# Loading v of batches 0 and 1 in place, w_out by row pairs, and a new set of priorities in a fused attention and feed-forward kernel

## The chip, the cores and the metric

The kernel runs on one core of a Trainium2 chip. It is timed in device microseconds (us) for one execution, inputs and outputs in the chip's memory. A second number is the span of a profiled execution, from the program's first instruction to its last. The engines are named PE (TensorE matmuls), PEld (its weight loads), DVE (VectorE), ACT (ScalarE), POOL (GpSimd) and SP (SyncE). POOL and SP here mostly issue DMAs: POOL the loads that convert float32 to bfloat16, SP the stores, the DMA transposes and two plain loads.

## The reference

There are 8 batches of 8 heads, 576 positions and 64 features. Heads 0 to 3 attend to the last 32 positions; heads 4 to 7 attend to every fourth position of the last 128. The result, as 4608 rows of 512, goes through a feed-forward block.

```python
scores = scale * np.matmul(q, k.transpose(0, 1, 3, 2))
mask_plain = (rel >= 0) & (rel < window)                                    # window 32
mask_dil = (rel >= 0) & (rel < window * dilation) & (rel % dilation == 0)   # dilation 4
attn = softmax(np.where(mask, scores, -1e9))
x = np.matmul(attn, v).transpose(0, 2, 1, 3).reshape(B * S, H * D)
a = x @ w1            # w1, w2: 512 x 1024
b = x @ w2
h = a * b @ w3        # w3: 1024 x 1024
out = h @ w_out       # w_out: 1024 x 512
```

## The kernel before

**Algebra.** The two last products are made one: `w3 @ w_out` is computed once on the chip into `wf_sb`, in eight parts. A part is a load of 128 rows of w3, eight PE transposes of it ("W3T", `w3_back`), an ACT copy to `w3T`, eight matmuls against `wo_sb` ("W3M", `w3_mul`) and a copy to `wf_sb` ("W3D").

**Attention.** A batch has two units u: the plain heads (u=0) and the dilated ones (u=1), and each has six blocks of 96 queries. q and k are loaded by rows (`load_rows`, a contiguous run for each partition) and turned on DVE in 32x32 blocks into `qt` and `kt` (`turn`, "Tqn", "Tkn"). For scores ("S"), 8 small matmuls per block go to PSUM. In batch 0 four groups of three blocks are formed, and the mask is added by four matmuls against `bias` ahead of each; from batch 1 on a group has five blocks and DVE multiplies by a mask ("M"). ACT takes the exponentials ("E"). A step is half a unit: 12 matmuls of `et` with v and a column of ones ("V"), a reciprocal ("R"), a normalization ("N"), and a way back to feature-major order in `XT`. For batches 0 and 1 that way is six PE transposes ("X", `back`) and a copy ("K", `keep`); later it is a DMA transpose on SP.

**v.** `vps` are two buffers of 128 partitions: partitions 32 to 127 hold a block's 96 positions, and partitions 0 to 31 hold the 32 before them (the halo). From batch 2 on (`DIRECT_V = 2`) one DMA for the plain heads and eight for the dilated ones load v straight into place, 256 bytes of float32 at a time (`load_v_plain`, `load_v_dil`), and one DVE copy fills the halo (`halo_v`). For batches 0 and 1 v comes by rows, is turned on DVE, transposed on PE in four parts of six transposes ("VT", `v_back`) and copied to `vps` ("VK", `v_keep`).

**Feed-forward.** A unit of 288 rows is half a batch. For each of eight 128-wide slices f of d_ff come four matmuls for a and four for b ("UP", line 563), an ACT copy of a and a DVE product into `gt` (line 578). For each 128 rows of output eight matmuls follow ("DOWN", line 589), a copy and a store. The first sixteen slices alternate: slices 0 to 3 of units 0 and 1, then slices 4 to 7 of both.

**Order.** Every piece of work is a task with an engine, an assumed duration, dependencies and a priority. `Plan.run` plays these through once as the program is built, and the resulting order is fixed for each engine. Durations and priorities therefore change nothing but the order. If PE would be idle in that play before its first UP, it gets filler matmuls ("fill", line 701). Loads go out on POOL in the order of `B0_LOADS`, then `FIRST_LOADS`, then by batch; POOL also builds the masks (`MASK_AT` sets their place among the loads). Completion semaphores of POOL's loads are used in turn, eight of them: a load is issued when the eighth one before it has landed. q and k of batch 0, u=0, are loaded by SP as float32 into `gt` and rounded by ACT (`round_rows`, "C").

Of the kernel before, what the change touches and what calls it, by code (L numbers as in the profile page):

```python
# [10 lines left out]
P = 128  # L11
# [19 lines left out]
LATE = False  # L31
TURNED = 2
DIRECT_V = 2
ORDER = (2, 3, 0, 1)
RES = (0, 2, 1, 3)
RANK = dict(E=0.5, VK=3, K=2, N=0.2, T=0.5, VT=0.05, S=0.1, V=0.05, X=0.1, W=0.5, C=5)
FIRST = {"E": 3, "VK": 1, "K": 0.2, "N": 2, "T": 0.2, "VT": 0.05, "S": 0.3, "V": 0.1, "X": 0.3}
WARM = 25
FILL = 110
FIRST_LOADS = ("30", "w0", "v10", "w1", "w2", "31", "k10", "q10", "o0", "o1", "32", "33", "34", "q11", "k11", "v11", "35", "36", "37")  # L40
SHIFT = {}
ON_DVE = ("K0.2", "VK0.1.1", "W3D1", "W3D4", "W3D5")
GRP = 5
WHOLE = ("qn", "kn")
B0_LOADS = ("v0", "q1", "k1", "v1")
HALVED = ("K0.0", "K0.1", "K0.3", "K1.1", "VK0.0.0", "VK0.1.0", "VK1.0.1", "VK1.1.0")
MASK_AT = 19.5
PARTED = 0
BUSY = 4500
LEAD = 1.1  # L50
# [13 lines left out]
class Plan:  # L64
# [15 lines left out]
    def run(self):  # L80
# [42 lines left out]
        while len(order) < n:  # L123
            progress = True
            while progress:
                progress = False
                for e in engines:
# [31 lines left out]
                    else:  # L159
                        t.end = free[e] = now + t.dur  # L160
# [26 lines left out]
def kernel(  # L187
# [75 lines left out]
    def round_rows(nm, u, half):  # L263
# [14 lines left out]
        nc.scalar.copy(out=o, in_=i)  # L278
# [26 lines left out]
    def halo_v(b):  # L305
        vp = vps[b % 2]
        nc.vector.tensor_copy(out=vp[0:32, :, 1:6, 0:D], in_=vp[96:128, :, 0:5, 0:D])
# [6 lines left out]
    def load_wo(c):  # L314
        g = slice(4 * c, 4 * c + 4)
        nc.gpsimd.dma_start(
            out=wo_sb[:, g, :],
            in_=moe_w_out[512 * c : 512 * (c + 1), :].rearrange("(a p) f -> p a f", p=P),
        )
# [155 lines left out]
    class Step:  # L475
# [51 lines left out]
        def back(self):  # L527
            self.x = bank(6 * QB, BF16)
            for i in range(6):
                nc.tensor.transpose(  # L530
                    out=self.x[:, i * QB : (i + 1) * QB],
                    in_=self.xo[0:QB, i * P : (i + 1) * P],
                    identity=ident[0:QB, 0:QB],
                )
# [109 lines left out]
    def w3_back(ft):  # L644
        x = bank(KFF * P, BF16).rearrange("p (g x) -> p g x", g=KFF)
        for g in range(KFF):
            nc.tensor.transpose(  # L647
                out=x[:, g, :], in_=w3n[ft][:, g * P : (g + 1) * P], identity=ident
            )
# [70 lines left out]
    def loads_rows(nm, b, us=None):  # L720
# [4 lines left out]
        t = load(f"L{nm}{b}", 700, 3100 if us is None else 1600, old,  # L725
# [4 lines left out]
    def loads_v(b):  # L730
        old = vdone.get(b - 2, [])
        LV[b] = [load(f"LP{b}", 1300, 4700, old, lambda: load_v_plain(b))]
        LV[b] += [
            load(f"LD{b}.{m}", 600 if m % 3 != 1 else 1200, 770, old, lambda m=m: load_v_dil(b, m))
            for m in range(6)
        ]

    WC = (slice(0, 256), slice(256, 512), slice(512, 1024))

    def loads_w12(c):  # L740
        return [
            load("LW", 800, (1700, 1700, 3300)[c], [], lambda d=d, s=s: load_w(d, s, WC[c]))
# [3 lines left out]
    for i, nm in enumerate(WHOLE):  # L746
        t = add(f"LF{nm}", "SP", 100, [], lambda nm=nm: load_whole(nm, rows_of[nm], 0), -9 + i,
                lat=4400 + 1350 * i)
        L[(nm, 0, 0)] = [
            add(f"C{nm}.{half}", "ACT", 650, [t], lambda nm=nm, h=half: round_rows(nm, 0, h),  # L750
                -9 + i + 0.1 * half, lat=100)
            for half in range(2)
        ]
    plan.dma = 1200 + 1350 * len(WHOLE)
    for x in B0_LOADS:
        loads_rows(x[0] + "n", 0, (int(x[1]),))
# [10 lines left out]
    for x in FIRST_LOADS:  # L767
# [3 lines left out]
        elif x[0] == "o":  # L771
            lwo[c] = load(f"LWO{c}", 600, 3300, [], lambda c=c: load_wo(c))
        elif x[0] == "3":
            lw3[c] = load(f"LW3.{c}", 550, 1400, [], lambda ft=c: load_w3(ft))
        elif x[0] == "v" and DIRECT_V <= c:
            loads_v(c)
# [21 lines left out]
    def turns(b, u, nm, pr):  # L798
# [4 lines left out]
        else:  # L803
            parts = (2, 3, 4, 5) if b == 0 else (0, 1)
# [16 lines left out]
    for b in range(B):  # L821
# [9 lines left out]
        for u in range(2):  # L831
# [3 lines left out]
            for half in range(2):  # L835
# [6 lines left out]
                eng, dur = ("DVE", 980) if name in ON_DVE else ("ACT", 880)  # L842
                ways = [(eng, dur, slice(0, 4))]
                if name in HALVED:
                    ways = [("ACT", 540, slice(0, 2)), ("DVE", 560, slice(2, 4))]
                vals[(b, u, half)] = [
                    add(name, e, dur, [x, c0],
                        lambda b=b, u=u, h=half, e=e, hs=hs: v_keep(b, u, h, e, hs),
                        10 * b + rank("VK", b), lat=100)
                    for e, dur, hs in ways  # L850
                ]
        if b >= DIRECT_V:
            hal = add(f"HALO{b}", "DVE", 820, LV[b] + [c0], lambda b=b: halo_v(b), 10 * b + 2,
                      lat=80)
            for u in range(2):
                for half in range(2):
                    vals[(b, u, half)] = [hal] + LV[b]


        def group(blocks, biased):  # L860
# [6 lines left out]
            if biased:  # L867
                s = add("S" + n, "PE", 980, need + [blk, idt], lambda: g.scores(True),
                        b - 99 + rank("S", b), slot=4)
                e = add("E" + n, "ACT", 1150, [s], g.exps, 10 * b + rank("E", b), lat=100, after=old)  # L870
# [30 lines left out]
        while steps < 4 * B:  # L901
# [14 lines left out]
            if (bb, i) == (0, 2) and LATE:  # L916
                for t in late:
                    t.after.append(vv)
                    t.deps.append(vv)
            rc = add(f"R{n}", "DVE", 240, [vv], st.recip, 10 * bb + rank("N", bb), lat=0,  # L920
                     after=prev["x"][i])
            ns = [
                add(f"N{n}", "DVE", 960 if u == 0 else 555, [vv, rc],
                    lambda st=st, part=part: st.norm(part), 10 * bb + rank("N", bb), lat=80)
                for part in ((None,) if u == 0 else (0, 1))
            ]
            if bb < TURNED:
# [4 lines left out]
                if name in HALVED:  # L932
                    ways = [("ACT", 400, slice(0, 3 * QB)), ("DVE", 270, slice(3 * QB, 6 * QB))]
                x = [
                    add(name, e, dur, [x], lambda st=st, e=e, c=c: st.keep(e, c),
                        10 * bb + rank("K", bb), lat=100)
                    for e, dur, c in ways
                ]
# [9 lines left out]
    def ups(k, f):  # L948
# [4 lines left out]
        wl = lw12[(0, 0, 1, 1, 2, 2, 2, 2)[f]]  # L953
# [98 lines left out]
```

The softmax here doesn't subtract the row's maximum and nothing guards it: scores larger than these inputs give would overflow.

## Time and profile before

| what | value |
|---|---|
| median of 3 runs | 254.99 us (254.92 to 255.07) |
| the profiled execution's own time | 255.02 us |
| its span | 253.2 us |
| granted PE clock | 0.998 |
| PE busy | 245.8 us, 97% of the span |
| PEld, DVE, ACT, POOL busy | 67%, 66%, 49%, 27% |
| UP matmuls (L563), 1024 of 128x288 | 136.3 us busy, 286 ns each |
| DOWN matmuls (L589), 280 of 128x512 | 65.8 us busy, 379 ns each |
| v transposes on PE (L412), 48 | 3.5 us busy, 219 ns each |
| filler matmuls (L701), 23 | 3.6 us busy |
| read from HBM | 38.80 MB |

Matmuls overlap, so the mean duration of one is longer than the step from one to the next. Where steps matter, they are read from the starts in the timeline or from the pieces of the chain of work that ended last. PE's busy time includes fillers, and a matmul is pipelined, so 97% does not mean that 97% is useful. Data rates in the profile count the bytes written, which for a converting load is half of what is read.

### The profile page before, as it was taken

The page shows a single profiled execution, that of the slowest core. Times are in us where ns is not written, and L with a number is a line of the kernel's source. Part 1 is how long each engine was busy: PE and PEld are TensorE (multiplying, and loading weights), DVE is VectorE, ACT ScalarE, POOL GpSimd, SP SyncE. Part 2 cuts the span into 40 slices and gives each one's busy share as a digit, 9 for nine tenths or more (in the row PEclk, how much of TensorE's full clock was granted, in tenths as well). Part 3 has the DMA queues.
Part 4 walks back from the last instruction along what each step waited for, and adds up shares of the span by engine and source line. Part 5 has one row for each costly group of instructions (what it writes and reads, how often), then busy time and mean ns, then how long its engine had stood idle before and what let it go on. Part 6 is the DMA issues. An engine that isn't in the chain of part 4 may idle for free.

```text
span 253.2 us, 6818 instructions
## 1 busy us (share of the span) xinstructions
PE 245.8 (97%) x2760; PEld 170.6 (67%) x2760; DVE 167.9 (66%) x350; ACT 124.3 (49%) x221; POOL 67.8 (27%) x106
## 2 busy tenths in 40 slices
PE   7889999999999999999999999999999999999994
PEld 5668876565767676677676766676767666777662
DVE  3998657697898887588868977837737365333321
ACT  5664555766635534362626526356353643333331
POOL 7635835343614432303250310800000000000000
PEclk9999999999999999999999999999999999999999
DMA  7999999999997999998799667862332223311114
GB/s 226 204 200 209 207 210 211 208 107 184 220 168 121 189 170 208 235 95 114 122 202 110 89 77 104 137 84 65 67 65 67 67 67 67 104 36 51 41 41 124
DMA packets 59422, 33.40 MB, mean 132 GB/s; under 512 B 44800, under 2 KB 49280, under 8 KB 59392
## 3 DMA queue, kind: packets, MB, share of 16 engines
q0 software_dynamic: 38592, 18.81, 58.7%
q1 hardware_dynamic: 20656, 14.10, 24.3%
q8 instruction: 21, 0.34, 0.6%
q14 instruction: 9, 0.07, 0.1%
q10 hardware_dynamic: 144, 0.07, 0.1%
HBM read 38.80 MB, written 9.44 MB: 190 GB/s over the span
## 4 chain that ended last, share of the span: by engine, by line
PE 90%; DVE 5%; DMA 2%; issue 1%; ACT 1%; ACTq 0%; DVEq 0%
PE ps L563 49%; PE ps L589 24%; PE ps L659 6%; PE ps L490 4%; PE ps L454 4%; DMA gt<-in_q_dram 2%; DVE qt L403 1%; DVE xo L513 1%; PE ps L647 1%; PE ps L607 1%; PE ps L701 1%; PE ps L530 1%; ACT qn L278 0%; DVE et L473 0%; PE ps L412 0%
## 5 line engine op out<-in xcount | busy, mean ns | idle before, releaser
L563 PE MATMUL ps<-XT,w_sb 128*128 128x288 bf16 x1024 | 136.3, 286 | 0.0
L563 PEld LDWEIGHTS <-w_sb 128*128 128x128 bf16 x1024 | 97.8, 98 | 30.6
L578 DVE TENSOR_TENSOR gt<-ps,asb 128x288 bf16<-128x288 f32 x128 | 57.5, 454 | 49.0 <-PE ps L563 46.7
L573 ACT CAST asb<-ps 128x288 bf16<-128x288 f32 x128 | 50.7, 398 | 49.3 <-PE ps L563 46.0
L589 PE MATMUL ps<-wf_sb,gt 128*128 128x512 bf16 x280 | 65.8, 379 | 0.0
L600 ACT COPY osb<-ps 128x512 f32<-128x512 f32 x35 | 20.5, 585 | 55.1 <-PE ps L589 55.0
L589 PEld LDWEIGHTS <-gt 128*128 128x128 bf16 x280 | 27.2, 98 | 26.9
L300 POOL DMA_DIRECT2D vp<-in_v_dram x48 | 30.3, 639 | 48.3 <-PE ps L490 30.3
L465 ACT ACTIVATE et<-ps 128x1920 bf16<-128x1920 f32 (+2 forms) x21 | 34.2, 1633 | 7.7 <-PE ps L454 5.5
L513 DVE TENSOR_TENSOR xo<-ps,rcp 96x384 bf16<-96x384 f32 (+1 forms) x48 | 31.4, 675 | 0.5
L473 DVE TENSOR_TENSOR et<-et,mask 128x960 bf16<-128x960 bf16 (+1 forms) x34 | 21.2, 645 | 6.8 <-ACT et L465 6.7
L403 DVE STREAM_TRANSPOSE qt<-qn 128x320 uint32<-128x320 uint32 (+3 forms) x34 | 22.3, 670 | 2.1 <-ACT qn L278 1.8
L490 PEld LDWEIGHTS <-et 128*128 128x128 bf16 x384 | 14.6, 98 | 1.9 <-issue 0.4
L490 PE MATMUL ps<-vp,et 128*128 128x65 bf16 x384 | 15.5, 193 | 0.1
L659 PE MATMUL ps<-wo_sb,w3T 128*128 128x512 bf16 x64 | 15.0, 379 | 0.1
L403 DVE STREAM_TRANSPOSE kt<-kn 128x320 uint32<-128x320 uint32 (+3 forms) x18 | 11.6, 646 | 4.5 <-PE ps L454 4.3
L454 PEld LDWEIGHTS <-kt 32*128 32x128 bf16 x768 | 9.1, 92 | 5.9 <-issue 4.7
L454 PE MATMUL ps<-qt,kt 32*128 32x96 bf16 x768 | 12.1, 201 | 0.7 <-DVE kt L388 0.7
L501 DVE RECIPROCAL rcp<-ps 96x12 f32<-96x12 f32 x32 | 6.9, 218 | 8.3 <-PE ps L490 8.0
L286 POOL DMA_DIRECT2D vp<-in_v_dram x6 | 7.2, 1194 | 11.5 <-PE ps L490 10.7
L659 PEld LDWEIGHTS <-w3T 128*128 128x128 bf16 x64 | 5.9, 98 | 6.3 <-issue 0.3
L388 DVE STREAM_TRANSPOSE kt<-kn 128x576 uint32<-128x576 uint32 (+1 forms) x9 | 9.9, 1121 | 0.2 <-PE ps L454 0.2
(56 smaller groups left out, 117.6 us busy)
## 6 DMA issues: line engine op xcount, KB each, us to landing
qn<-in_q_dram POOLq DMA_DIRECT2D x6, 576.0 KB, 8.2
kn<-in_k_dram POOLq DMA_DIRECT2D x6, 576.0 KB, 9.0
w3n<-in_moe_w_dram POOLq DMA_DIRECT2D x8, 256.0 KB, 11.2
out_dram<-osb SPq DMA_DIRECT2D x7, 256.0 KB, 3.0
out_dram<-osb SPq DMA_DIRECT2D x8, 224.0 KB, 2.9
vp<-in_v_dram POOLq DMA_DIRECT2D x6, 288.0 KB, 9.2
out_dram<-osb SPq DMA_DIRECT2D x8, 192.0 KB, 2.9
out_dram<-osb SPq DMA_DIRECT2D x8, 160.0 KB, 3.2
```

The source lines that it names most:

```text
L300: nc.gpsimd.dma_start(out=vp[32 + p0 : 32 + p0 + n, 4:8, m, 0:D], in_=v_rows(b, 4, 4 * t0 + res, [[4 * D, n], [S * D, 4], [1, D]]),)
L403: nc.vector.transpose(out=o, in_=i)
L454: nc.tensor.matmul(out=self.sp[:, g, QB * i : QB * i + QB], lhsT=kt[prt, u, QB * m : QB * m + P, c], rhs=qq, start=(c == 0 and not biased) ...
L465: nc.scalar.activation(out=ev, in_=self.sp[:, :, 0:x], func=ACT.Exp, scale=scale)
L473: nc.vector.tensor_tensor(out=ev, in0=ev, in1=mk, op=AL.mult)
L490: nc.tensor.matmul(out=self.o[:, g, mm, :], lhsT=grp.et[:, c0 : c0 + P], rhs=vps[self.b % 2][:, 4 * self.u + g, 3 * self.hf + mm, 0 : D + ...
L513: nc.vector.tensor_tensor(out=dst, in0=self.o[0:QB, hs, :, 0:D], in1=self.rcp[0:QB, hs, :].unsqueeze(3).to_broadcast([QB, n, 3, D]), op=AL ...
L563: nc.tensor.matmul(out=held[(key, k, f)], lhsT={"a": w1_sb, "b": w2_sb}[key][:, c, f * P : (f + 1) * P], rhs=unit_cols(k, c), start=(first ...
L573: nc.scalar.copy(out=a_sb, in_=held[("a", k, f)])
L578: nc.vector.tensor_tensor(out=gt[:, f, c0 : c0 + UNIT].rearrange("p (r m t) -> p m r t", r=2, m=BLK), in0=held[("b", k, f)].rearrange("p ( ...
L589: nc.tensor.matmul(out=y, lhsT=gt[:, f, c0 : c0 + P], rhs=wf_sb[:, f, :], start=(f == 0), stop=(f == KFF - 1),)
L659: nc.tensor.matmul(out=o, lhsT=w3T[ft][:, g, :], rhs=wo_sb[:, g, :], start=(g == 0), stop=(g == KFF - 1),)
```

## The change

1. v of batches 0 and 1 is loaded in place as well (`DIRECT_V = 0`), in three parts that can be ordered apart: "p" (plain heads, 288 KB written), "a" and "b" (two dilated halves, 144 KB each). A step waits for its own part, and the halo copy is split accordingly into three DVE copies, "HP", "HA" and "HB". The row loads of v, their turns, the VT transposes and the VK copies of these batches go.
2. `load_wo` reads two adjacent rows of w_out per partition (4 KB in place of 2 KB). Row order inside a 256-row stretch changes, so `w3_back` transposes every second column of w3 to match.
3. Loads come in another order, and the planner gets other durations, ranks and about 90 single shifts of priority (`SHIFT`, empty before). `Plan.run` lets a DVE or ACT task overlap its successor by 70 or 90 ns. The masks come earlier among the loads.
4. The two roundings of q (Cqn) go from ACT to DVE, other K copies change engine, and the normalization of u=1 in batches 0 and 1 is one instruction in place of two. The first a and b products are cut in two, plain heads first (`PARTED = 2`). With `LATE` the last score group of batch 0 is ordered behind the third V of batch 0.

```diff
-LATE = False
+LATE = True
 TURNED = 2
-DIRECT_V = 2
+DIRECT_V = 0
...
-RANK = dict(E=0.5, VK=3, K=2, N=0.2, T=0.5, VT=0.05, S=0.1, V=0.05, X=0.1, W=0.5, C=5)
-FIRST = {"E": 3, "VK": 1, "K": 0.2, "N": 2, "T": 0.2, "VT": 0.05, "S": 0.3, "V": 0.1, "X": 0.3}
+RANK = dict(E=1, VK=3, K=3, N=0.2, T=0.3, VT=0.3, S=0.2, V=0.05, X=0.4, W=3, C=5)
+FIRST = {"E": 1, "VK": 1, "K": 2, "N": 0.5, "T": 0.3, "VT": 0.3, "S": 0.2, "V": 0.2, "X": 0.05}
...
-FIRST_LOADS = ("30", "w0", "v10", "w1", "w2", "31", "k10", "q10", "o0", "o1", "32", "33", "34", "q11", "k11", "v11", "35", "36", "37")
+FIRST_LOADS = ("w0", "w1", "30", "q10", "w2", "31", "o0", "32", "o1", "a1", "33", "34", "k10", "p1", "q11", "k11", "35", "36", "37", "b1")
...
-ON_DVE = ("K0.2", "VK0.1.1", "W3D1", "W3D4", "W3D5")
+QUARTERS = ("qn",)
+ON_DVE = ("Cqn.0", "Cqn.1", "K0.1", "K0.2", "K0.3", "K1.1", "K1.2", "VK0.1.1", "VK1.0.0", "VK1.1.0", "VK1.1.1", "W3D2", "W3D6")
...
-B0_LOADS = ("v0", "q1", "k1", "v1")
-HALVED = ("K0.0", "K0.1", "K0.3", "K1.1", "VK0.0.0", "VK0.1.0", "VK1.0.1", "VK1.1.0")
-MASK_AT = 19.5
-PARTED = 0
+B0_LOADS = ("q1", "k1", "p0", "a0", "b0")
+HALVED = ("K0.2", "K0.3", "K1.0", "K1.1", "K1.2", "VK0.0.0", "VK1.1.0", "VK1.1.1")
+MASK_AT = 16.5
+WCUT = (256, 512)
+PARTED = 2
+OVERLAP = {"DVE": 70, "ACT": 90}
 BUSY = 4500
-LEAD = 1.1
+LEAD = 1.2
...
-        nc.scalar.copy(out=o, in_=i)
+        if eng == "ACT":
+            nc.scalar.copy(out=o, in_=i)
+        else:
+            nc.vector.tensor_copy(out=o, in_=i)
...
-    def halo_v(b):
-        vp = vps[b % 2]
-        nc.vector.tensor_copy(out=vp[0:32, :, 1:6, 0:D], in_=vp[96:128, :, 0:5, 0:D])
+    def halo_v(b, hs=slice(0, 8), ms=slice(1, 6)):
+        vp, old = vps[b % 2], slice(ms.start - 1, ms.stop - 1)
+        nc.vector.tensor_copy(out=vp[0:32, hs, ms, 0:D], in_=vp[96:128, hs, old, 0:D])
...
         nc.gpsimd.dma_start(
-            out=wo_sb[:, g, :],
-            in_=moe_w_out[512 * c : 512 * (c + 1), :].rearrange("(a p) f -> p a f", p=P),
+            out=wo_sb[:, g, :].rearrange("p (s j) f -> p s j f", j=2),
+            in_=moe_w_out[512 * c : 512 * (c + 1), :].rearrange(
+                "(s p j) f -> p s j f", p=P, j=2
+            ),
         )
...
-                out=x[:, g, :], in_=w3n[ft][:, g * P : (g + 1) * P], identity=ident
+                out=x[:, g, :], in_=w3n[ft].rearrange("p (s x j) -> p s j x", x=P, j=2)[:, g // 2, g % 2, :],
+                identity=ident,
             )
...
+        elif b >= DIRECT_V:
+            lp, la, lb = (LV[b][x] for x in "pab")
+            h0 = add(f"HP{b}", "DVE", 450, lp + [c0],
+                     lambda b=b: halo_v(b, slice(0, 4), slice(1, 6)), 10 * b + rank("VK", b), lat=80)
+            h1 = add(f"HA{b}", "DVE", 220, la + [c0],
+                     lambda b=b: halo_v(b, slice(4, 8), slice(1, 3)), 10 * b + rank("VK", b), lat=80)
+            h2 = add(f"HB{b}", "DVE", 300, la + lb + [c0],
+                     lambda b=b: halo_v(b, slice(4, 8), slice(3, 6)), 10 * b + rank("VK", b), lat=80)
+            vals[(b, 0, 0)] = vals[(b, 0, 1)] = [h0] + lp
+            vals[(b, 1, 0)] = [h1] + la
+            vals[(b, 1, 1)] = [h2] + la + lb
```

The order in which the two built programs' instructions stand shows the rest. On PE, before the first UP, the program has 25 warming matmuls and 12, 8 and 9 fillers (with 6 and 3 more between the first UPs), where the one before has 7, 4, 1, 2, 6 and 3. On POOL, nine direct loads of v stand ahead of the first load of w1. On ACT and DVE the copies and turns of v are gone.

## The prediction

> **What bounds the kernel now.** I read the page first (busy shares, slices, chain by engine), then who made PE wait, PE's and DVE's timelines of the first 62 us, and the data rate by stretch.
>
> ```profile
> PE 245.8 (97%) x2760; PEld 170.6 (67%) x2760; DVE 167.9 (66%) x350; ACT 124.3 (49%) x221; POOL 67.8 (27%) x106
> ...
> DMA  7999999999997999998799667862332223311114
> ...
> PE 90%; DVE 5%; DMA 2%; issue 1%; ACT 1%; ACTq 0%; DVEq 0%
> ```
>
> PE is the bound, and DMA is busy without a break in the first half of the slices. The list of PE's waits shows how little waiting there is:
>
> ```profile
> PE ps L684 <- DVE warm L688: 1.4, 1, 1.4
> PE ps L454 <- DVE kt L388: 0.7, 1, 0.7
> PE ps L437 <- DVE xo L513: 0.5, 1, 0.5
> ```
>
> The largest is at the very start. But fillers hide idle time, so the start has to be read from PE's timeline (start, length, line, shape, count):
>
> ```profile
> 18.64 1.11 PE L701 MATMUL ps<-warm 128*128 128x256 bf16 x6
> 19.58 0.53 PE L490 MATMUL ps<-vp,et 128*128 128x65 bf16 x12
> 19.95 0.49 PE L701 MATMUL ps<-warm 128*128 128x256 bf16 x3
> 20.27 1.63 PE L563 MATMUL ps<-XT,w_sb 128*128 128x288 bf16 x12
> 21.74 0.42 PE L530 MATMUL ps<-ident,xo 96*128 96x96 bf16 x6
> 22.00 1.64 PE L563 MATMUL ps<-XT,w_sb 128*128 128x288 bf16 x12
> 23.47 0.83 PE L412 MATMUL ps<-ident,vt 128*128 128x128 bf16 x12
> 24.14 5.06 PE L563 MATMUL ps<-XT,w_sb 128*128 128x288 bf16 x40
> ```
>
> Steps from start to start: UP 4.90/40 = 0.1225 us, VT 0.67/12 = 0.056, X 0.26/6 = 0.043, V 0.37/12 = 0.0305. The chain of work gives DOWN and W3M 1.73/8 = 0.216 and S 0.55/40 = 0.0137 (plus 0.1 after each group); W3T is 0.45/8 = 0.056. After 22.00 us, when the last X of batch 0 is through, the program before still has 1012 UP (124.0), 280 DOWN (60.5), 64 W3M (13.8), 336 V (10.25), 672 S with 17 group ends (10.9), 56 W3T (3.1), 24 VT (1.35), 24 X (1.0): 224.9 us. That puts the last half tile (L607) at 246.9; the chain has it at 247.76. So only 0.8 us is lost in the last 230: all that can be won is work taken off PE, and an earlier end of the start. The last 5.5 us (L607 1.76, then copy and store) are untouched.
>
> [...] Direct v writes 128 B pieces, and the stretch of batch 2's v stands out beside one of row loads (columns: busy PE, PEld, DVE, ACT, POOL, clock, DMA share, GB/s):
>
> ```profile
> 46.00:50.00 4.00, 4.00 (x64) 2.14 (x62) 1.53 (x4) 2.53 (x3) 1.56 (x3) 1.00 1.11 212
> 50.00:54.00 4.00, 3.92 (x62) 3.01 (x60) 3.92 (x9) 3.93 (x5) 0.92 (x2) 1.00 2.07 158
> ```
>
> Within the second, the part that is v alone runs at about 150 GB/s. [...] VT reads its weights with a stride of two elements, W3T densely, and both load in 98 ns. W3T with stride two therefore costs nothing. [...] No DVE cast from SBUF is in this trace[...].
>
> **The change, part by part.**
>
> *PE work.* 48 VT go: 2.7 us. Half lie before 22.00, among fillers. Counted from the same point (last X of batch 0 done), the changed order has 1008 UP (four more came earlier, -0.5), 64 W3T (+0.45), no VT (-1.35), the rest unchanged: 223.55 us. That is 1.4 us less, if nothing new waits. Turns of v (four pairs or singles, 5.6 us of DVE) and the v copies (7.6 us of ACT and DVE) go; they hide behind PE after 22 us and matter only in the start.
>
> *The end of the start, T.* Before, T = 22.00. After, in the built order and with this trace's durations:
> - q lands at 4.8, k at 6.2 (SP, unmoved). Cqn on DVE: [...] ([...] ACT took 0.73 and 0.61). I take 0.5: done 5.9. The q turns (pair 1.3) 7.2. Then k halves and quarters of q of u=1, which are queued between them: 0.55 + 0.42 + 0.55, done 8.7. Before it was 8.6, so the first scores are no earlier.
> - Two score groups, two E (1.08 each): 11.5. The third group needs k of u=1 (lands 9.0, since v no longer stands ahead of q1 and k1): quarter 0.42, k pair 1.28, quarter 0.35 by 11.1, E done 12.7.
> - v: plain part landed about 11.0 (below), HP 0.45, HA 0.2: 11.8. Three V at 11.7, 12.05, 12.8, where the trace has 12.47, 14.16, 14.93. Here the VT part of the path is cut.
> - DVE: R 0.2, N 0.93, R 0.2, then HB. HB waits for the last dilated part (13.6), and N of the other plain step, K, R and N of the third are queued behind it: 0.25 late, then 14.9, 15.35, 16.5.
> - PE: X, 8 fillers, X, 9 fillers, the fourth score group (0.9) to 17.1, X 17.35, 4 UP, 6 fillers, V (its E ends 18.35) 18.85, 3 fillers, 12 UP 19.2 to 20.65, X. T = 20.9; with 0.7 for each Cqn, 21.3. I take 21.1.
>
> So the start brings 0.9 and less PE work 1.4: 2.3 us, before what the loads do.
>
> *Loads.* Times are the stream's, 288 KB by rows at 205 GB/s = 1.4 us. q1, k1 land at 7.6 and 9.0. Then 576 KB of v at 150 GB/s take 3.9 (by rows 2.9): plain 11.0, last dilated 13.0. With eight semaphores in turn, the eleventh load (last of v) is issued only when the third (plain) has landed. In this trace the last such load of batch 2 took 2.5 from issue to landing, so it lands at 13.6, and the stream has a hole of about 0.5. w0 and w1 (1024 KB, 512 B pieces, 197 GB/s) 5.3, w3 1.25, q 1.4, w2 2 x 2.55, next w3 1.25: landed at 27.9, and 28.3 by the trace's own intervals (w0 to w2 10.8, not 10.4). PE needs that w3 (W3T1) 0.45 + 56 x 0.1225 = 7.3 after T, so T cannot count as earlier than 20.6 to 21.0. The next needs are no tighter: w3.2 (3.8 later; due T + 11.2) 20.5 to 20.9, the second w_out half 19.8 to 20.2, w3.5 and w3.6 20.0 to 20.6. The kernel before had slack here (second w_out half landed 34.6, used from 38.25). The masks, 4.75 us on POOL, now stand ahead of the last w2 load, which is issued at about 21.5; its turn in the stream comes at 24.5, so this is hidden while the masks end before 23.
>
> *w_out by row pairs.* 28 to 34 us, with 1 KB pieces written, ran at 207 GB/s, 38 to 48 with 2 KB at 211: 1 MB in 4.97 in place of 5.07. Worth 0.1 of a stream, at most 0.3 by single landings.
>
> *Priorities after 60 us.* PE loses 0.3 us there now, so reordering can only cost. In the new order XT of batch 2 is due at 90.5 and its last early V ends at 79.6; the DMA transposes took 7.5 from issue to landing, so they fit. I put 0 to 1.5 us, taken 0.3 with the loads' errors.
>
> **Sum.** Span = 21.1 + 223.55 + 0.8 + 5.5 = 250.95; plus 0.3: 251.2. The profiled execution took 255.02 at a span of 253.2, 1.8 more, and the median is 254.99. Predicted: 253.0 us, a gain of 2.0.
>
> **Rivals.**
> - *Full gain.* [...] the hole absent, v at 158 GB/s or better: T = 20.5 and no load late. Span 250.2, time 252.0; with some of the 0.8 gone 251.2. For it: all loads are FIFO and the start has slack at V. Against: fillers and the fourth score group fix PE's order.
> - *The loads become the bound and eat most of it.* w2 and w3.1 arrive 1 to 2 us later than worked out (hole of 1.5, or v at 120 GB/s, which makes 4.9 of 3.9): T counts as 22.3 to 23, time 254.2 to 254.9. For it: the gate is already level with T; every us late is a us lost. Then the change seems to do nothing.
> - *Slower.* The eight semaphores starve the stream: nine small parts of v hold the ring while each load of w waits for one of them and then for its own start-up of about 2 us. The place is 11 to 15 us; it decides from 2.8 us of lost stream on (0.4 now in the sum), since the gain over the gate is 2.4. At 4 us lost the time is 256.7. Against it: from the twelfth load on issues are 0.75 apart and transfers 1.3.
> - *It doesn't do what it says:* the row pairs, most likely true of them; 0.1 us.
>
> **How the numbers follow.** Likeliest case 0.55: 252.3 to 253.9. Full gain 0.17: 251.0 to 252.3. Loads eat most 0.17: 253.9 to 255.4, of which 0.07 within 0.2% (254.5 to 255.5, about what a measurement here can tell from no change). Slower 0.11: above 255.5. Faster is 0.55 + 0.17 + 0.10 = 0.82. The range leaves out the lower third of the full gain and the slow case: 251.4 to 255.2.
>
> **What would show it.** Right: no VT group; three V of batch 0 by 13.3; last X of batch 0 near 21; the first W3T after 56 UP waits little, if at all, on w3; v's stretch near 11 us with a rate of about 150 GB/s; w_out's two loads still about 2.5 us apart; total PE count 48 less apart from fillers. Wrong: T near 22 or later with DVE's HB or the fourth E ahead of it; waits of PE on DMA of w or w3 of over 1 us at 24 to 32 us; new waits after 60 us of more than 1 us together.

## The result and the profile after

The changed kernel takes **262.61 us** (median; 261.86 to 263.76), the kernel before, on the same chip, 255.03 (254.92 to 255.15). The ratio is 1.0301, with a 95% interval of 1.0257 to 1.0346: slower by 7.6 us, where 253.0 was forecast. The profiled execution took 262.02 at a span of 260.2. Executions more than 1.5% above the fastest of the same kernel are left out of every median and ratio of this document: two of six of b1_direct (261.6 and 262.7), five of 22 of b1_halo_early (258.8 to 260.8), one of six of b1_tuned (258.0) and two of six of b1_tuned_2 (258.0 and 258.1).

The page of the kernel after has these lines in place of those of before:

```profile
PE 243.0 (93%) x2695; PEld 168.9 (65%) x2727; DVE 161.5 (62%) x339; ACT 119.7 (46%) x213; POOL 78.2 (30%) x120
...
PE   7798999899999787999989999999999999999994
...
DMA  7999999999999999979998719762415032212113
...
PE 58%; DMA 27%; POOL 8%; issue 4%; DVE 0%; POOLq 0%; ACT 0%; DVEq 0%; ACTq 0%
```

PE does less (2727 weight loads for 2760 before; 32 matmul records are missing here, so its busy time reads a little low), but its row of slices has gaps at the 14th to 16th digit (about 85 to 104 us), and the chain of work that ended last runs through DMA for 27% of the span, 2% before. The list of waits names what PE stood for, and adds one of DVE that did not exist before (total us, times, longest):

```profile
DVE vp L314 <- DMA vp<-in_v_dram: 9.0, 5, 3.2
PE ps L574 <- DVE gt L589: 4.2, 3, 1.9
PE ps L658 <- DMA w3n<-in_moe_w_dram: 2.1, 3, 0.9
...
PE ps L574 <- DMA XT<-xo: 1.1, 1, 1.1
```

L314 is the halo copy of v, L589 the a times b product, L574 UP, L658 the turn of w3. The start is as forecast. PE's timeline (start, length, line, shape, count, and the idle time ahead with what ended it):

```profile
21.24 0.42 PE L541 MATMUL ps<-ident,xo 96*128 96x96 bf16 x6
22.45 0.62 PE L658 MATMUL ps<-ident,w3n 128*128 128x128 bf16 x8 [0.79 <-DMA w3n<-in_moe_w_dram]
22.91 7.02 PE L574 MATMUL ps<-XT,w_sb 128*128 128x288 bf16 x56
30.30 0.62 PE L658 MATMUL ps<-ident,w3n 128*128 128x128 bf16 x8 [0.36 <-DMA w3n<-in_moe_w_dram]
```

The last X of batch 0 is through at 21.24 + 6 x 0.043 = 21.5; T was put at 21.1, and before it was 22.0. The loss is later. DVE's timeline and PE's, near 85 us:

```profile
81.62 0.45 DVE L589 TENSOR_TENSOR gt<-ps,asb 128x288 bf16<-128x288 f32 x1
85.24 1.08 DVE L314 COPY vp<-vp 32x2560 bf16<-32x2560 bf16 x1 [3.17 <-DMA vp<-in_v_dram]
86.35 0.76 DVE L413 STREAM_TRANSPOSE qt<-qn 128x320 uint32<-128x320 uint32 x1
86.96 0.43 DVE L589 TENSOR_TENSOR gt<-ps,asb 128x288 bf16<-128x288 f32 x1
```
```profile
87.45 3.10 PE L574 MATMUL ps<-XT,w_sb 128*128 128x288 bf16 x24 [1.94 <-DVE gt L589]
...
97.52 4.08 PE L574 MATMUL ps<-XT,w_sb 128*128 128x288 bf16 x32 [1.06 <-DMA XT<-xo]
103.28 0.65 PE L574 MATMUL ps<-XT,w_sb 128*128 128x288 bf16 x4 [1.68 <-DVE gt L589]
```

DVE reaches batch 3's halo copy at 82.07 and waits 3.17 us for v. A product that PE needs is queued behind the copy, and PE waits 1.94 for it. The same happens with batch 4 (2.69 us of DVE, 1.68 of PE) and batch 5 (2.05 of DVE, 0.60 of PE). In the kernel before the copy comes at a later place and waits for nothing:

```profile
90.34 0.82 DVE L307 COPY vp<-vp 32x2560 bf16<-32x2560 bf16 x1
```

So two things moved: the landing of v and the place of its first user. v of a batch comes in nine transfers, and the copy doesn't need the ninth, which fills the last block. By the trace's landing times the eighth of batch 3 lands at 76.7 before and at 85.0 after (the ninth at 86.3 after; the trace of before doesn't tell it); the copy's place went from 90.3 to 82.1. Before, there were 13.7 us of room; after, the place is 2.9 us ahead of the landing.

### The profile page after: what moved, and what is told of

It reads as the page before. It is cut to its first block, busy times and chain, and to the rows that moved or that the text cites. A ratio compares the mean times of both kernels' runs of the same rounds, so it can differ in the third digit from the quotient of the medians.

```text
span 260.2 us, 6711 instructions
## 1 busy us (share of the span) xinstructions
PE 243.0 (93%) x2695; PEld 168.9 (65%) x2727; DVE 161.5 (62%) x339; ACT 119.7 (46%) x213; POOL 78.2 (30%) x120
## 4 chain that ended last, share of the span: by engine, by line
PE 58%; DMA 27%; POOL 8%; issue 4%; DVE 0%; POOLq 0%; ACT 0%; DVEq 0%; ACTq 0%
PE ps L574 35%; PE ps L600 17%; DMA vp<-in_v_dram 15%; DMA wo_sb<-in_moe_w_out_dram 5%; DMA w3n<-in_moe_w_dram 4%; DMA qn<-in_q_dram 4%; PE ps L500 3%; PE ps L464 2%; POOL mask L377 2%; POOL w_sb L317 2%; POOL qn L256 1%; POOL w3n L335 1%; POOL kn L256 1%; PE ps L618 1%; POOL vp L307 1%
## 5 line engine op out<-in xcount | busy, mean ns | idle before, releaser
L574 PE MATMUL ps<-XT,w_sb 128*128 128x288 bf16 x1024 | 135.4, 286 | 5.3 <-DVE gt L589 4.2
L574 PEld LDWEIGHTS <-w_sb 128*128 128x128 bf16 x1024 | 97.8, 98 | 34.9 <-issue 6.0
L589 DVE TENSOR_TENSOR gt<-ps,asb 128x288 bf16<-128x288 f32 x128 | 57.0, 452 | 49.4 <-PE ps L574 46.8
L600 PE MATMUL ps<-wf_sb,gt 128*128 128x512 bf16 x252 | 63.4, 379 | 1.3
L307 POOL DMA_DIRECT2D vp<-in_v_dram x64 | 40.2, 636 | 53.5 <-PE ps L500 18.0
L483 DVE TENSOR_TENSOR et<-et,mask 128x960 bf16<-128x960 bf16 (+1 forms) x34 | 21.3, 639 | 9.4 <-ACT et L475 9.3
L671 PE MATMUL ps<-wo_sb,w3T 128*128 128x512 bf16 x60 | 14.4, 379 | 0.3 <-ACT wf_sb L682 0.2
L293 POOL DMA_DIRECT2D vp<-in_v_dram x8 | 9.9, 1233 | 14.9 <-PE ps L574 10.0
L314 DVE COPY vp<-vp 32x2560 bf16<-32x2560 bf16 (+3 forms) x12 | 8.4, 704 | 9.3 <-DMA vp<-in_v_dram 9.0
L413 DVE STREAM_TRANSPOSE kt<-kn 128x320 uint32<-128x320 uint32 (+1 forms) x16 | 11.3, 704 | 2.2 <-PE ps L464 2.1
L256 POOL DMA_DIRECT2D kn<-in_k_dram x9 | 5.9, 658 | 16.0 <-DVE kt L413 14.4
```

The lines of the kernel that those rows point to most:

```text
L307: nc.gpsimd.dma_start(out=vp[32 + p0 : 32 + p0 + n, 4:8, m, 0:D], in_=v_rows(b, 4, 4 * t0 + res, [[4 * D, n], [S * D, 4], [1, D]]),)
L413: nc.vector.transpose(out=o, in_=i)
L483: nc.vector.tensor_tensor(out=ev, in0=ev, in1=mk, op=AL.mult)
L574: nc.tensor.matmul(out=held[(key, k, f)], lhsT={"a": w1_sb, "b": w2_sb}[key][:, c, f * P : (f + 1) * P], rhs=unit_cols(k, c), start=(first ...
L589: nc.vector.tensor_tensor(out=gt[:, f, c0 : c0 + UNIT].rearrange("p (r m t) -> p m r t", r=2, m=BLK), in0=held[("b", k, f)].rearrange("p ( ...
L600: nc.tensor.matmul(out=y, lhsT=gt[:, f, c0 : c0 + P], rhs=wf_sb[:, f, :], start=(f == 0), stop=(f == KFF - 1),)
```

## The experiments

Two theories. **Order:** the new planning places what uses v ahead of its landing. **Stream:** v in place makes the row of loads late. A third, that the hole in the stream at 12 to 14.5 us is the cause, was tried along with them.

**Row pairs alone.** The kernel before with the edits of `load_wo` and `w3_back` only.

> The kernel before with only w_out by row pairs and the matching stride in the w3 transposes. Prediction: the same within 0.2%, w_out's two loads 0.0 to 0.3 us closer together. Rival: weight loads with a stride of two cost PE time (64 of them in the filled stretch), 255.5 us or more.

Measured: 254.96, ratio 0.9999 (0.9990 to 1.0007). The row pairs do nothing that can be measured, and are out. The weight loads of W3T take 98 ns in the profile of before, where they read densely, and 98 in that of after, with a stride of two.

**The halo copies moved, the hole filled, both.** After, with the planned start of some tasks changed once the plan is made:

```diff
     order, _ = plan.run()
+    at = {t.name: t for t in order}
+    for b in range(2, B):                    # halo_late, both
+        at[f"HALO{b}"].start = min(at[f"V{b}.{i}"].start for i in range(4)) - 2000
+    at["HB0"].start = at["V0.3"].start - 900  # hole_filled, both
+    first_w = [t for t in order if t.name == "LW"][1].start
+    for m in (3, 4, 5):
+        at[f"LD0.{m}"].start = first_w + 10 * m
+    order.sort(key=lambda t: t.start)
```

> The changed kernel, with only the halo copies of batches 2 to 7 moved later in DVE's order (2 us, in the planned times, ahead of the first V of their batch); loads, PE, ACT and POOL orders as they are. Theory A (the halo copies of batches 3, 4 and 5 stand in DVE's order before their v has landed; DVE holds the products behind them and PE runs out): the 7.9 us that DVE waited on v loads at these three goes, PE's 4.2 us of waits on DVE's products and the 1.1 on a DMA transpose go with it: 256 to 258 us. Theory B (the loads as such are late, and PE waits for them wherever the copy stands): the wait moves to the V of batch 3 on PE, 261 to 263 us.

> The changed kernel, with two of the four loads of w0 and w1 issued ahead of the last third of v of batch 0, and the last halo copy of batch 0 moved in DVE's order to just before the V that needs it. Theory C (the small parts of v fill the eight semaphores, so that the stream of loads runs dry at 12 to 15 us and everything after it lands some 2 us later): the first w part lands near 13.5 in place of 16.3, the first w3 near 20 in place of 22.4, PE's 2.6 us of waits on w3 go, v of batch 3 lands 2 us or more earlier; with the halo copies where they are that takes 2.6 us for certain and part of the late 5: 257 to 260 us. Rival (the stream is short of rate, not of issues, and only swaps who is late): the landings of w3 move by less than 0.5 us, 261.5 to 263 us.

> Both moves together. A and C together: PE waits on w3 and on DVE products gone, 253.5 to 255.5 us. If A and C are two names of one cause (late v of batch 3), no better than the better of the two alone by more than 0.5 us.

Measured: halo_late 261.35, ratio 1.0235 (1.0215 to 1.0256); hole_filled 263.84, 1.034 (1.0279 to 1.040); both 259.23, 1.017 (1.011 to 1.023).

The hole is not the cause by itself: in hole_filled the first part of w1 lands at 13.6 in place of 16.3 and the first part of w3 at 21.0 in place of 22.4, but v of batch 3 no earlier than after (87.5, its ninth transfer), and the time is not shorter. PE's wait for w3 at 22 us is gone, and one for w3 near 50 us has grown from 0.95 to 1.92. With the copies moved too, filling it comes out 2.1 us better (both against halo_late), but the two intervals overlap. halo_late lies in the range of theory B, though not by its mechanism: PE waits at no V of batch 3. Moving the halo copies takes the waits for `gt` away, but little time comes back, for two reasons that the lines of halo_late show. The wait moves on, to a DMA transpose of XT, which after had only waited 1.1 for:

```profile
91.68 3.62 PE L600 MATMUL ps<-wf_sb,gt 128*128 128x512 bf16 x16
97.37 6.24 PE L574 MATMUL ps<-XT,w_sb 128*128 128x288 bf16 x36 [2.08 <-DMA XT<-xo]
```

And those 36 UP take 6.24, 0.173 each, where 0.1225 is the step elsewhere. The view by windows shows a lower clock under them (length; busy PE, PEld, DVE, ACT, POOL; granted PE clock; DMA share; GB/s):

```profile
93.00:95.00 2.00, 2.00 (x11) 0.94 (x10) 2.00 (x6) 0.58 (x1) 0.20 (x1) 1.00 1.14 208
95.00:97.00 2.00, 0.30 (x2) 0.02 (x1) 2.00 (x3) 0.58 (x1) 0.57 (x1) 1.00 1.63 146
97.00:99.00 2.00, 1.63 (x11) 1.22 (x11) 1.13 (x3) 0.40 (x1) 0.00 (x0) 0.84 1.58 213
99.00:101.00 2.00, 2.00 (x11) 1.23 (x9) 0.54 (x2) 0.40 (x1) 0.00 (x0) 0.50 1.85 153
101.00:103.00 2.00, 2.00 (x15) 1.49 (x14) 0.49 (x2) 0.73 (x2) 0.15 (x1) 0.81 1.58 185
```

After PE's wait of 2.08 us the granted clock was 0.84, 0.50 and 0.81 in the three last windows: what they lack of full clock adds up to 1.7 us, as much as 3.4 us at 0.50 would lack. The 36 UP took 1.83 more than 36 steps of 0.1225.

**The old planning, v by rows, v said to land later, batch 1 alone.** Four kernels. old_priorities is after with the ranks, shifts, engines, durations, overlaps and load order of before, and the short durations kept for v of batches 0 and 1 (it does the normalization of the dilated heads in two parts, as before, while the way back expects one, so some heads of batches 0 and 1 end in each other's place; the work is the same). The three others:

```diff
 # v_by_rows: after
-DIRECT_V = 0
+DIRECT_V = 2
-FIRST_LOADS = ("w0", "w1", "30", "q10", "w2", "31", "o0", "32", "o1", "a1", "33", "34", "k10", "p1", "q11", "k11", "35", "36", "37", "b1")
+FIRST_LOADS = ("w0", "w1", "30", "q10", "w2", "31", "o0", "32", "o1", "33", "34", "k10", "v10", "q11", "k11", "v11", "35", "36", "37")
-B0_LOADS = ("q1", "k1", "p0", "a0", "b0")
+B0_LOADS = ("q1", "k1", "v0", "v1")
 # v_said_later: after, in loads_v
+        for t in [t for ts in LV[b].values() for t in ts]:
+            t.lat = {0: 0, 1: 0, 2: 3000}.get(b, 10000)
 # b1_direct: before (short v durations for b < 2)
-DIRECT_V = 2
+DIRECT_V = 1
-FIRST_LOADS = ("30", "w0", "v10", "w1", "w2", "31", "k10", "q10", "o0", "o1", "32", "33", "34", "q11", "k11", "v11", "35", "36", "37")
+FIRST_LOADS = ("30", "w0", "w1", "w2", "31", "k10", "q10", "o0", "o1", "32", "33", "34", "q11", "k11", "v11", "35", "36", "37")
```

> Loads of v in place as after, row pairs as after, but the load durations, ranks, shifts, engines and the order of the loads as before (only for the direct v of batches 0 and 1 the short durations stay). Theory order (the new planning puts what uses v too early; the loads themselves do little harm): no DVE wait on v of batches 2 and up over 0.5 us, PE waits of under 1 us in all after 60 us, time 252.5 to 254.5. Theory stream (v in place slows the whole row of loads, and that is the loss, whatever the order): v of batch 3 lands at 80 us or later again (before 73 to 77), PE waits over 3 us in all on DMA, time 256 to 259.

> After with v of batches 0 and 1 by rows and turned again, all of the new planning kept. The planner makes the start longer (53 fillers in place of 38; last X of batch 0 planned 4.5 us later), and 24 more turns on PE come after it (1.35 us), so 5 to 6 us are to be had on top in any case. Theory stream: v of batch 3 lands by 77 us, the waits on v and of PE after 60 us are gone (6.6 us won), time 261 to 262. Theory order: DVE still waits on v of batches 3 to 5 for more than 4 us in all and PE for the product behind it, time 264 to 268.

> After, with the planner told that v of batch 2 lands 3 us later and v of batches 3 and up 10 us later than it assumes; no load is moved in the list, only what comes after v. Theory order: DVE's waits on v fall from 9 us to under 1, the transposes wait less than in the run with the halo copies alone moved, time 256 to 258.5. Theory stream: the waits turn up at other loads or transposes (over 3 us of PE in all after 60 us), time 260 to 262.5.

> The kernel before with v of batch 1 alone in place, nothing else. 24 turns on PE less, all after 22 us where PE is the bound: 1.35 us. Theory order: the loads behind it come some 1.5 us later and this has room, time 253.4 to 254.0 (ratio 0.994 to 0.996). Theory stream: the loads behind it eat the gain, PE waits over 1 us on DMA after 40 us, time 254.8 to 256.

Measured:

| run | time | ratio | last X of batch 0 starts | v of batch 3 landed (ninth transfer) |
|---|---|---|---|---|
| after | 262.61 | 1.0301 (1.0257 to 1.0346) | 21.24 | 86.3 |
| old_priorities | 261.97 | 1.0305 (1.0271 to 1.0338) | 24.31 | 88.3 |
| v_by_rows | 262.95 | 1.0308 (1.0280 to 1.0337) | 26.14 | 79.1 |
| v_said_later | 259.24 | 1.0163 (1.0131 to 1.0194) | | 88.5 |
| b1_direct | 258.80 | 1.0132 (1.0097 to 1.0166) | | 82.9 |

old_priorities misses both numbers. Its waits on v of batch 2 and later are gone, as theory order has it, but the old ranks do not suit the direct start: the last X comes 3.1 us later, PE having waited 2.2 for w3 ahead of it. It separates nothing by its time. In v_by_rows the last X comes 4.9 us later than in after, with 1.4 us more of UP and w3 turns done by then, and PE turns 1.35 us more; yet it ends only 0.3 later: some 4.5 us were won elsewhere, with v landing 7 us earlier and one wait on it left (2.2 us). That is near what stream said, though above its 262. v_said_later wins 3.4 us with the loads as late as ever (88.5): that is what order said, though less than its number; its halo copy is now placed so late (93.65) that PE waits 1.7 for it. Each theory is right in part.

b1_direct was the surprise, and fits neither theory's number. One batch of v in place, in a kernel that had no waits there, costs 3.4 us by the ratio, and PE's waits are not on DMA. PE's timeline has two short waits (the halo copy of batch 1 stood on DVE behind a copy that itself waited for PE; then the normalization behind that), and the windows show the clock again:

```profile
49.53 0.49 PE L490 MATMUL ps<-vp,et 128*128 128x65 bf16 x11 [1.02 <-DVE vp L307]
49.87 0.61 PE L647 MATMUL ps<-ident,w3n 128*128 128x128 bf16 x8
52.15 0.66 PE L530 MATMUL ps<-ident,xo 96*128 96x96 bf16 x6 [1.67 <-DVE xo L513]
```
```profile
50.00:52.00 2.00, 0.47 (x9) 0.30 (x6) 1.66 (x3) 1.21 (x2) 1.54 (x3) 0.76 1.13 220
52.00:54.00 2.00, 1.85 (x24) 1.86 (x25) 0.65 (x2) 0.90 (x2) 0.21 (x1) 0.50 1.09 207
54.00:56.00 2.00, 1.83 (x26) 1.78 (x25) 1.57 (x4) 0.83 (x2) 0.36 (x1) 0.50 1.60 183
56.00:58.00 2.00, 1.95 (x5) 0.76 (x5) 0.77 (x2) 0.94 (x1) 0.57 (x1) 0.53 2.42 160
58.00:60.00 2.00, 2.00 (x20) 1.19 (x19) 1.27 (x3) 0.94 (x2) 0.59 (x1) 1.00 0.95 58
```

The waits are 2.7 us; the windows lack 3.4 us of full clock, as much as 6.8 us at 0.50 would lack. This execution took 259.34 with a mean clock of 0.983; the fastest of the same kernel, with 1.000, took 256.32, which is the 254.96 of the kernel before, less the 1.35 of the turns, plus the waits.

**A stall made on purpose, and its price.** The kernel before, where the first normalization of batch 1 is done four times:

```diff
-                    lambda st=st, part=part: st.norm(part), 10 * bb + rank("N", bb), lat=80)
+                    lambda st=st, part=part, again=3 * (n == "1.0"): [
+                        st.norm(part) for _ in range(1 + again)
+                    ], 10 * bb + rank("N", bb), lat=80)
```

> The kernel before with the first normalization of batch 1 (0.95 us on DVE) done four times over, the same values each time. The way back that waits for it had 0.9 us of room, so PE waits about 1.9 us once, near 54 us. Theory stall costs its length: granted clock 1.0 throughout, time 256.5 to 257.2. Theory stall also cuts the clock (as seen in the run with v of batch 1 alone in place): clock about 0.5 for some 6 us after it, 3 us more, time 259 to 260.5.

Measured: 257.26, ratio 1.0089 (1.0074 to 1.0103): 2.27 us more, where the profiled execution shows a wait of 2.08. Four of five executions took 257.22 to 257.26, with a clock of 0.998 to 1.000. The fifth, the profiled one, took 258.91 at a mean clock of 0.993, and these windows show where it was lower:

```profile
44.77 0.43 PE L530 MATMUL ps<-ident,xo 96*128 96x96 bf16 x6 [2.08 <-DVE xo L513]
```
```profile
44.00:46.00 2.00, 1.23 (x19) 1.24 (x20) 1.99 (x3) 0.77 (x2) 0.99 (x2) 0.86 1.09 203
46.00:48.00 2.00, 2.00 (x10) 0.98 (x8) 1.95 (x4) 1.70 (x2) 0.77 (x2) 0.50 1.13 215
48.00:50.00 2.00, 2.00 (x9) 0.82 (x8) 1.17 (x2) 0.48 (x1) 0.34 (x1) 0.79 1.10 211
```

So this wait of 2.08 us cost about its length in four executions (2.23 to 2.27 us over the kernel before), and 1.7 more in the one where the clock dropped to 0.50. Neither theory had it quite: the lower clock came in one execution of five.

**Less to load.** After without the loads of three parts of w3, 3.8 us of the stream at 47 us; their turns read the fifth part again. repaired joins v_said_later with the last part ("b") of v of batch 0 loaded behind the first parts of w1 and w2.

```diff
 def load_w3(ft):
+        if ft > 4:
+            w3n[ft] = w3n[4]
+            return
```

> After without the loads of the last three parts of w3 (their turns read the fifth part again, so a part of the product is wrong): 3.8 us of the row of loads go at about 47 us, nothing else is moved. Theory stream (the row of loads is late, and what waits, waits for that): v of batch 3 lands at 81 to 82 in place of 85, DVE's waits on v fall from 9.0 us to under 2, PE's waits after 60 us from 5.3 to under 2, time 257 to 259. Theory buffers (the loads of batch 3 and on start when their buffers come free, so an earlier row gives nothing): v of batch 3 lands at 84 or later, time 261 to 263.

> After with the planner told that v of batches 2 and up lands later (3 and 10 us, as in the run before this), and the last third of v of batch 0 loaded behind the first w1 and w2 parts. If the losses of the two places add: 259.2 less 1 to 2, 257 to 258.5. If the loads late by then set the end in any case: 259 to 260.5. Neither theory expects it below 256.

Measured: three_w3_less **256.04**, ratio 1.0042 (1.0028 to 1.0055); repaired 260.93, 1.0232 (1.0218 to 1.0245), worse than v_said_later alone, with new waits of PE, 1.3 us for exponentials and 2.8 for one product near 68 us. Of the 7.6 us lost, 3.8 us less of loads give 6.6 back, where theory stream had 257 to 259; PE's wait of 0.95 near 50 us, for one of the parts left out, goes too. v of batch 3 lands at 81.3 with its eighth transfer (85.0 after), and the halo copy goes at 81.61 without a wait. The list of waits:

```profile
PE ps L661 <- DMA w3n<-in_moe_w_dram: 1.1, 2, 0.7
...
DVE vp L314 <- DMA vp<-in_v_dram: 1.1, 3, 0.5
PE ps L577 <- DMA XT<-xo: 0.8, 1, 0.8
...
PE ps L577 <- DVE gt L592: 0.8, 1, 0.8
```

The waits on v (1.1 us) are those of batches 0 and 1. Theory buffers falls: the later loads do come earlier when the stream is shorter.

**Only the load durations.** The kernel before, the same loads and matmuls (and nine fillers more, by the new plan), with the planner's shorter durations (v plain 4700 to 2500, a dilated part 770 to 380, rows 3100 to 2850, and so on). b0_alone is after with v of batch 1 by rows again.

> The kernel before with the planner's shorter load durations alone; every load and every matmul is the same. The planner now orders the halo copies of batches 2 to 4 about 9 us earlier or more and adds 9 fillers at the start. Theory both needed (late loads and an order without room): v of batch 3 lands at about 77 as before, its halo copy waits under 0.5 us, that of batch 4 (planned at 90.5, landing 91 to 93) 1 to 3, time 255.5 to 258. Theory order alone: waits on v of over 4 us in all and PE behind them, time 259 to 263.

> After with v of batch 1 by rows and turned again, batch 0 in place, all else of the new planning kept: 24 turns more on PE (1.35 us), the row of loads about 2 us shorter by 52 us. If half of the lateness is batch 1's: v of batch 3 lands near 82 to 83, waits on v fall to about half of the 9 us, time 260 to 262.5. If nearly all of the lateness is batch 0's and the start's: v of batch 3 lands at 84 or later, time 263 to 265.

Measured: short_loads_said **265.19**, ratio 1.040 (1.0385 to 1.0414); b0_alone 266.02, 1.0465 (1.0409 to 1.0520). The durations alone, with no batch of v moved to direct loads, cost 10.2 us. v of batch 3 lands at 78.4 and its copy (82.8) does not wait. Batch 4's does:

```profile
90.00 0.44 DVE L578 TENSOR_TENSOR gt<-ps,asb 128x288 bf16<-128x288 f32 x1
96.16 0.96 DVE L307 COPY vp<-vp 32x2560 bf16<-32x2560 bf16 x1 [5.71 <-DMA vp<-in_v_dram]
97.15 0.66 DVE L473 TENSOR_TENSOR et<-et,mask 128x960 bf16<-128x960 bf16 x1
```
```profile
97.86 0.36 PE L490 MATMUL ps<-vp,et 128*128 128x65 bf16 x6 [4.29 <-DVE et L473]
98.80 1.12 PE L490 MATMUL ps<-vp,et 128*128 128x65 bf16 x17 [0.58 <-DVE et L473]
```

PE stands 4.9 us there, the clock is at 0.62 and 0.53 in the four microseconds after it (1.7 us), and the start is 2.5 us longer (last X of batch 0 at 24.27). With 0.7 for w3 that is 9.8 of the 10.2. Before, the same copy came at 109.89, behind a landing at 91.4 of the transfer that it needs. That landing is at 96.0 here, where the new order has also put a load of q ahead of it; a copy at 109.89 would still have had room. Theory order alone is the nearer one, and its range (259 to 263) was still too low.

b0_alone misses both numbers. v of batch 3 lands at 81.8 and the waits on v are 1.1 us, as the first theory had it, but PE waits six times for exponentials, masks and products between 63 and 74 us (0.5 to 0.9 each) and once 2.5 for a product near 93. Why the plan with batch 1 by rows fits so badly there was not followed up. For less_and_said (three_w3_less with v_said_later):

> After without the loads of the last three parts of w3 (a part of the product is wrong, as in the run before with that edit alone, 256.0), and with the planner told that v of batches 2 and up lands 3 and 10 us later. If late loads and the places of what waits for v are the whole loss: the 1 to 2 us of waits that were left after 60 us go too, time 253.5 to 255. If something else costs as well (the order of the other work, the clock): 255.5 to 258.

Measured: 257.38, ratio 1.0094 (1.0081 to 1.0107). Nothing is left of waits on v of batches 2 and up that PE feels, but a w3 part at 22 us costs 1.8, and scores and products at 65 to 68 us 1.4. The two causes are not the whole.

**v in place where its users have room.** b1_direct again, with the order mended by hand. In b1_halo_early the halo copy of batch 1 goes ahead of the DVE copy that it stood behind, and the first normalization ahead of a mask. In b1_tuned_2 the whole step goes ahead of a w3 product:

```diff
     order, _ = plan.run()
+    at = {t.name: t for t in order}
+    first = at["W3M4"].start
+    ahead = ("W3D3", "HALO1", "S1.1.2", "V1.0", "E1.1.2", "R1.0", "N1.0", "M1.1.2.0", "M1.1.2.1")
+    for i, name in enumerate(ahead):
+        at[name].start = first - 90 + 10 * i
+    at["X1.0"].start = first + 10
+    at["W3M4"].place, at["W3T5"].place = 0, 3
+    order.sort(key=lambda t: t.start)
```

b1_tuned is the same without "W3D3"; there X1.0 overwrites a w3 product in PSUM before its copy, and the instructions are otherwise the same.

> The kernel before with v of batch 1 in place, and batch 1's halo copy ordered on DVE ahead of the copy of the fifth w3 product (it stood behind it, and PE then waited 1.0 for it and 1.7 for the normalization behind that), the first normalization ahead of the mask. Theory order: both waits go, and with them the cut of the granted clock after them; 24 turns less on PE: time 253.2 to 254.2, faster than before. Theory stream: loads that come about 3 us later than before make PE wait elsewhere after 60 us for over 1.5 us, time 254.8 to 257.

> The kernel before with v of batch 1 in place, and batch 1's halo copy, last scores, first product with v, exponentials, normalization and mask all ordered ahead of the fifth w3 product, whose 1.7 us then cover the 1.4 us of DVE between the product with v and its way back. If v in place is a gain once PE has cover there: the 0.9 us wait of the run with the halo copy alone moved goes, time 253.6 to 254.3, faster than before. If the loads that come late by then set the end: new waits of PE on DMA after 60 us, time 254.8 to 257.

> As the run b1_tuned, with one ACT copy of a w3 product put back ahead of the way back that takes its PSUM bank. If v in place is a gain once PE has cover there: 253.2 to 254.0, faster than before by 0.4 to 0.7%. If the loads that come late by then set the end: 254.8 to 257.

Measured: b1_halo_early 254.81, ratio 1.0003 (0.9989 to 1.0016); b1_tuned 253.48, 0.9939 (0.9926 to 0.9953); b1_tuned_2 **253.36, 0.9943 (0.9928 to 0.9957)**. In b1_halo_early PE still waited 0.9 for the normalization, with one turn of w3 (0.45 us) as its only cover; that ate the gain. With a product of 1.7 us as cover nothing waits:

```profile
46.08 0.54 PE L490 MATMUL ps<-vp,et 128*128 128x65 bf16 x12
46.46 1.89 PE L659 MATMUL ps<-wo_sb,w3T 128*128 128x512 bf16 x7
48.18 0.42 PE L530 MATMUL ps<-ident,xo 96*128 96x96 bf16 x6
```

The gain, 1.45 us by the ratio, is about that of 24 turns less at 0.056: 1.35. And the stream is as late as in the changed kernel: the eighth transfer of v of batch 3 lands at 86.0. The halo copy has its place behind it:

```profile
89.16 0.82 DVE L307 COPY vp<-vp 32x2560 bf16<-32x2560 bf16 x1
```

A landing at 86.0 costs nothing here, and one at 85.0 cost 3.17 us of DVE in the changed kernel. The execution of b1_tuned that took 258.0 was the profiled one, and its list of waits has one that b1_tuned_2's has not:

```profile
PE ps L563 <- DMA XT<-xo: 2.3, 1, 2.3
```

PE stands there near 117 us for a DMA transpose that took 12.6 us from issue to landing (6.3 for the same one in b1_tuned_2). Why it is late in one execution and not in another is open. So this version beats both kernels in its median, not in every execution.

## Why the prediction was wrong, by its steps

- **The start, T: right.** 21.5 for 21.1. Three V of batch 0 by 13.3, no VT, row pairs without effect: all as written. The two roundings of q on DVE took 0.67 and 0.66, not 0.5. The 0.5 was the author's estimate; no trace of the kernel before shows such a rounding on DVE. For 0.7 the prediction had 21.3.
- **"PE loses 0.3 us there now, so reordering can only cost ... I put 0 to 1.5 us, taken 0.3": this step failed.** From T to the end the profiled execution took 260.2 - 21.5 = 238.7 where the sum has 223.55 + 0.8 + 5.5 + 0.3 = 230.15. Of the 8.55 us over it, PE's waits after 60 us for products behind the halo copies and for XT are 4.2 + 1.1 = 5.3, against the 0.3 taken. Its waits on w3 are 2.1 (next point), and the other 1.1 is not traced to a wait. I looked at the XT of batch 2 and the last early V, and never at the halo copies of batches 3 to 5. The change cut the planner's durations for v nearly by half. The built order showed those copies at earlier places, and the profile of before had the landings to set against them.
- **The loads: mechanism right, size too small.** The sum has the last part of v of batch 0 at 13.6, with a hole of 0.5, and the four loads named w0 and w1 in 5.3 us behind it. v landed at 13.75, nearly as written, but those four took until 21.15, 7.4 us. The windows show the stream nearly at a stand (before, then after; columns as above):

```profile
12.00:14.00 2.00, 1.75 (x51) 1.45 (x49) 1.93 (x7) 1.58 (x2) 1.28 (x2) 1.00 1.41 199
```
```profile
12.00:14.00 2.00, 1.58 (x40) 1.34 (x37) 1.64 (x5) 0.91 (x1) 2.00 (x3) 1.00 0.65 37
```

So the w3 part at 30.3 landed at 30.25, some 2 us later than the 27.9 to 28.3 of the sum: the rival in which loads eat the gain. PE's waits on w3 came to 2.1 us. I took the later needs for slack, but the lateness goes on: q of batch 2 lands at 55.0 for 49.2 before, the eighth transfer of v of batch 3 at 85.0 for 76.7. Of the 5.8 us at q of batch 2 I estimate 2.1 from these four loads (7.4 less 5.3) and 2.0 from v of two batches in pieces of 128 bytes (twice the 3.9 less 2.9 of the sum; 144 GB/s from 8 to 12 us, 205 before); the rest is not traced.

- **The rivals.** The slower rival had the place wrong (11 to 15 us, through the ring of semaphores). The ring is in the profile: POOL waited 0.55 us ahead of the tenth load until the second (k) landed, and 1.29 ahead of the eleventh until the third (v, plain) did. But filling that place alone gave no time (263.84 in hole_filled). None put the price at the users of v behind 80 us.
- **A wait costs its length:** assumed throughout without being said. In some executions it cost more (1.7 us on top of 2.08 in one of norm_four), but the profiled one of the changed kernel had a clock of 1.00.

What stays open: how the 7.6 us divide between late loads and early places. They are not two shares of a sum, since either gives room to the same copies: a shorter stream gives 6.6 back, later places 3.4, both together 5.2. three_w3_less and less_and_said stay 1.0 and 2.4 us above the kernel before, with small waits at places that differ from plan to plan. Ranks, shifts and the moves between engines were never tried alone, so what they cost or bring by themselves is not shown.

## What to carry to other kernels

The order on each engine is fixed ahead, and here an instruction that waited for a DMA held what was queued behind it on its engine: the halo copy of batch 3 held DVE for 3.17 us, and PE waited 1.94 for the product behind it. So the number to read for each such instruction is its room: its place less the landing, in the profile of the kernel as it is, under its own load. Shorten an assumed load duration only by what the last part's landing allows where it is used, not by the rate of the stream where it runs undisturbed, and look again at the users two and three batches on: the lateness here was 5.8 us at q of batch 2 and 8.3 at v of batch 3. A step taken off the bound engine was a gain here only where what then came next had other work to cover its latency: the same edit gave +3.4, 0 and -1.4 us with three places of one step.

## What was not expected of the hardware

A wait of PE cost more than its length in some executions. After waits of 2.08 us (halo_late, and norm_four's fifth execution), of 4.29 and 0.58 (short_loads_said), and of 1.02 and 1.67 close together (b1_direct) the lowest granted clock in the windows of 2 us was 0.50, 0.50, 0.53 and 0.50. The windows lack 1.7 us of full clock in each of the first three and 3.4 in b1_direct. In windows of 1 us, b1_direct reads 1.00 up to 51 us, then 0.52, five times 0.50 and 0.57, and 1.00 again from 58 us on.

It did not come each time, and the length of the wait did not decide it here. norm_four had a mean of 0.998 to 1.000 in four executions of five. The profiled execution of the changed kernel has waits of 1.94, 1.06 and 1.68 at a clock of 1.00, while its other three had a mean of 0.991 to 0.993. A wait of 2.8 in the run both was followed by 1.00 (windows from 95 to 110 us), and after one of 2.8 in repaired, near 68 us, the page has 0.9 or more in every slice but the last. What decides it is not shown by these runs.
